# Turning the exponentials of attention tiles 6 to 11 by VectorE blocks and copies in a buffer of their own instead of by TensorE

## The chip, the cores and the metric

The kernel runs on one core of one Trainium2 chip. The metric is device time in microseconds, the median of repeated executions. Beside it there is one profiled execution, from which all rows below come. PE is TensorE, PEld its weight loads, DVE is VectorE, ACT is ScalarE, POOL is GpSimd, SP is SyncE, which starts the DMA transfers.

## What is computed

Three layers follow one another over 4608 tokens (8 batches of 576). All inputs are float32. Cut to what matters:

```python
k_p = k.reshape(B, H, Sp, 8, D).mean(axis=3)          # 72 pooled keys of 64 per head, 8 heads
v_p = v.reshape(B, H, Sp, 8, D).mean(axis=3)
scores = scale * (q @ k_p.T);  scores -= scores.max(-1)
attn = exp(scores);  attn /= attn.sum(-1) + 1e-09
x = (attn @ v_p)                                       # 4608 x 512

g = relu(x @ w_in) ** 2                                # 512 -> 2048
y = g @ w_out                                          # 2048 -> 512

logits = y @ phi                                       # 32 slots = 8 experts x 4
d = softmax(logits, over tokens);  slot_in = d.T @ y
slot_out[e] = relu(slot_in[e] @ w1[e]) @ w2[e]
out = softmax(logits, over slots) @ slot_out
```

## The kernel before

The tokens are cut into 36 tiles of 128. Work is written out in slots. A slot holds half a unit of the first product (`x @ w_in`): a unit is one tile and one quarter of the 2048 columns, twelve matmuls of line 492 in sequence, the high part of x, `xh`, times both parts of the weights and the low part, `xl`, times the high one. The function that emits a unit is `l1_steps`: twelve matmuls into a PSUM buffer of tag `l1` (two buffers), a relu on ScalarE out of PSUM into `r` (line 520), and a square, by VectorE from the PSUM buffer and `r` (line 528) or by ScalarE (line 530). The squared result `g` is stored to DRAM (line 532) and later read back in a turned form (line 572) for the logits (line 616) and their softmax (lines 658 to 743).

Attention of a tile is placed at slots fixed in advance, `attention(t, a_at[t])`: scores (`sc_steps`, matmuls of line 245, a row maximum by VectorE at line 253, and for most tiles eight exponentials with their sums by ScalarE at line 258), normalisation by VectorE (lines 285 to 287), turning (`att_aT` and `att_shift`, four and five slots behind the first), and the weighted sum (`av_steps`, line 340, then line 349 and line 351, which split it into `xh` and `xl`). The weighted sum takes the exponentials with the 72 keys in the partitions, `aT`, so that the normalised 128x(8x72) block `es` has to be turned for each of the eight heads. The kernel has two ways for this, and the set `EX` says which tiles take the second:

- by TensorE (`aT_steps`): eight transposes into PSUM (line 314), four heads in tag `gT` or `att` at a time, and two copies of 72x512 by ScalarE into `aT` (line 318);
- by blocks: VectorE turns all 32x32 blocks at once (line 328), reading `es` in columns of 96 for each head, into a 128x768 block; then twelve copies move the blocks to their places in `aT` (`att_shift`), by the pattern "VAVAVAAAVAVA" five of 32x256 and two of 8x256 on ScalarE (line 306), three and two on VectorE (line 308).

Tile pools hand out buffers: `aT` has one buffer, the 128x768 block lies in the last quarter of a `st1` buffer (`turned()[0]`). The other parts of that buffer and of `tmp` are five buffers for reloads of `g`, numbers 1 to 5 of the list `xbuf`. At the same time VectorE and ScalarE split the weights of the second matrix and pool keys and values; GpSimd pools them, too.

The order on each engine is made by the tile framework's scheduler from the slots and priorities, so that a change in one place can shift instructions of others.

Of the kernel before, what the change touches and what calls it, by code (L numbers as in the profile page):

```python
# [8 lines left out]
F32 = mybir.dt.float32  # L9
# [8 lines left out]
def kernel(  # L18
# [12 lines left out]
    nc = tc.nc  # L31
    B, H, S, D = q.shape
# [7 lines left out]
    P = 128  # L40
    NT = NTOK // P
# [29 lines left out]
    a1 = att_pools.enter_context(tc.tile_pool(name="a1", bufs=1))  # L71
# [217 lines left out]

    att_norm = whole(norm_steps)  # L290

    EX = range(12, NT)

    def att_shift(t):
        if t not in EX:
            return
        aT = aT_t[t] = a3.tile([SP, H, P], F32, tag="aT", name="aT")
        blk = turned()[0]
        for n in range(12):
            e = "VAVAVAAAVAVA"[n]  # L300
            r, m = n % 4, n // 4
            w = min(32, SP - 32 * m)
            dst = aT[32 * m:32 * m + w, :, 32 * r:32 * r + 32]
            src = blk[32 * r:32 * r + w, :, m]
            if e == "A":
                nc.scalar.copy(out=dst, in_=src)  # L306
            else:
                eng[e].tensor_copy(dst, src)  # L308

    def aT_steps(t, half):  # L310
        es = es_t[t]
        pa = ps("gT" if t in (0, 2, 4, 6, 8, 10, 12, 14, 16, 18, 20, 22, 24, 26, 28, 29, 30, 31, 33) else "att")
        for i in range(HH):
            nc.tensor.transpose(pa[:SP, i * P:(i + 1) * P], es[:, half * HH + i], ident)
        yield
        if t not in aT_t:
            aT_t[t] = a3.tile([SP, H, P], F32, tag="aT", name="aT")
        mark["aT", t] = nc.scalar.copy(
            out=aT_t[t][:, half * HH:(half + 1) * HH].rearrange("p h t -> p (h t)"), in_=pa[:SP]
        )  # L320
        yield

    def att_aT(t):
        if t in EX:
            es_t.pop(t)
            x = es2[t % 2]
            wide = bass.AP(tensor=x.tensor, offset=x.offset, ap=[list(x.ap[0]), [SP, H], [32, 3], [1, 32]])
            nc.vector.transpose(out=turned()[0], in_=wide)  # L328
            return
        for half in range(2):  # L330
            for _ in aT_steps(t, half):
                pass
# [212 lines left out]
            next(l1_t[t, j])  # L545

    xbuf, gT_at, g_back = [], {}, {}
    gT_free = [1, 2, 3, 4, 5]

    def turned():  # L550
        if not xbuf:
            x = stp.tile([P, 8, 512], F32, tag="st1", name="turned")
            xbuf.append(x[:, 6:8].rearrange("p a b -> p (a b)")[:, :H * 96].rearrange("p (h m i) -> p h m i", m=3, i=32))
            xbuf.extend(y[:, i:i + 2].rearrange("p a b -> p (a b)") for y, i in ((x, 0), (x, 2), (x, 4), (tmp, 0), (tmp, 2)))
        return xbuf

# [12 lines left out]
    def reload_turned(t, j):  # L569
        i = gT_at[t, j] = gT_free.pop(0)  # L570
        gc = gT_t[t, j] = turned()[i]
        nc.sync.dma_start(
            out=gc.rearrange("p (u f) -> p u f", u=2),
            in_=g_dram[t // 2][:, j].rearrange("u c (i s) f -> (c i) u (s f)", s=4),
        )
# [362 lines left out]
    def attention(t, a0):  # L938
        if t >= NT - 4:
            if t % 2 == 0:  # L940
                at(a0 - 2, pinned, "sq", turn_q, t)
            for n, fn in ((1, att_sc), (2, att_exp), (2, att_norm)):
                at(a0 + n, early, fn, t)
            n = (240, 242, 254, 259)[t - NT + 4]
            at(n - 2, early, att_aT, t)
            at(n - 1, early, att_shift, t)
            at(n, early, att_av, t)
            return
        if t < ND:
            at(a0, att_qT, t)  # L950
        elif t % 2 == 0:
            at(a0 - 2, pinned, "sq", turn_q, t)
        at(a0 + 1, att_sc, t)
        at(a0 + 2, att_exp, t)
        at(a0 + 2, att_norm, t)
        at(a0 + 4, att_aT, t)
        at(a0 + 5, att_shift, t)
        if a0 + 6 + t % 2 < 8 * ND + 14:
            at(a0 + 7, att_av, t)
        else:  # L960
            at(a0 + 6 + t % 2, pinned, "logits", att_av, t)
# [205 lines left out]
    for h in range(2):  # L1167
        cols = slice(h * QF // 2, (h + 1) * QF // 2)
        part = p2.tile([P, QF // 2], F32, tag="r", name="part")
        with tc.issue_after(mark["acc"].ins):  # L1170
            mark["acc"] = nc.vector.scalar_tensor_tensor(
                out=part, in0=acc[:, cols], scalar=scl, in1=dp[:, cols], op0=ALU.mult, op1=ALU.add
# [222 lines left out]
```

## Time and profile before

| | |
|---|---|
| median of 3 runs | 750.98 us (749.83 to 752.17) |
| the profiled execution | 751.86 us |
| its span, from first to last instruction | 750.1 us |
| mean granted clock of TensorE | 0.984 |
| TensorE busy | 715.6 us, 95% |
| VectorE busy | 524.3 us, 70% |
| ScalarE busy | 387.8 us, 52% |
| GpSimd busy | 136.5 us, 18% |

The busy times are those of the whole span. A busy share near 1 says that an engine has little room left, not that it is always the one waited for. A window cuts the span into stretches. In the chain of waits each piece was released by the one ahead of it, so that it shows who was waited for in each stretch. The granted clock is 1.00 at 2.4 GHz and 0.50 at 1.2 GHz.

### The profile page before, as it was taken

Reading aid. Unit: us, or ns where it says so; the run is one execution under the profiler, and the core shown is the slowest. Engines: PE = TensorE matmul, PEld = TensorE weight load, DVE = VectorE, ACT = ScalarE, POOL = GpSimd, SP = SyncE. Lnnn points to the kernel's source line nnn. Section 1 sums busy time; section 2 is a strip of 40 time slices with the busy share of each in tenths; the row PEclk is TensorE's granted clock in tenths of the full one; section 3 lists DMA queues with packets and bytes.
Section 4 is the critical chain, followed back from the end, with each engine's and each line's share of the span. In section 5 each row is a group of like instructions: output and inputs, shape, how many; then the busy total and the mean of one; then the engine's idle time right before and its main releaser. Section 6 shows DMA issues by size and latency. Waiting matters only on the chain.

```text
span 750.1 us, 13911 instructions
## 1 busy us (share of the span) xinstructions
PE 715.6 (95%) x4969; PEld 497.4 (66%) x4969; DVE 524.3 (70%) x1048; ACT 387.8 (52%) x1132; POOL 136.5 (18%) x151
## 2 busy tenths in 40 slices
PE   7799899999999999999999999999999999999985
PEld 7677678787776767666666656667666766764342
DVE  4998854497896788878979787778878574414132
ACT  3766767464656456346646462637466453333132
POOL 2234400004971400050342120320000000000000
PEclk9999999999999999999999999999999999999996
DMA  8967945658776996686998788879676434988998
GB/s 256 257 198 237 260 136 155 218 144 258 213 224 163 274 258 185 191 251 169 250 283 232 195 242 241 229 204 262 181 231 213 141 127 147 410 326 341 394 303 337
DMA packets 213012, 175.05 MB, mean 233 GB/s; under 512 B 75216, under 2 KB 169424, under 8 KB 212944
## 3 DMA queue, kind: packets, MB, share of 16 engines
q1 hardware_dynamic: 212944, 174.17, 75.7%
q8 instruction: 39, 0.64, 0.3%
q14 instruction: 29, 0.24, 0.1%
HBM read 126.94 MB, written 47.19 MB: 232 GB/s over the span
## 4 chain that ended last, share of the span: by engine, by line
PE 56%; DVE 19%; DMA 9%; ACT 6%; issue 5%; POOL 3%; SPq 1%; POOLq 0%; DVEq 0%; ACTq 0%
PE l L492 33%; PE misc L743 3%; ACT es L258 2%; DMA kv<-in_v_dram 2%; POOL w L429 2%; PE pl L616 2%; ACT aT L306 2%; DVE es L287 2%; DVE aT L308 2%; PE l L1228 2%; PE att L340 2%; DMA kv<-in_k_dram 2%; PE gT L340 2%; DMA tmp<-g_dram 1%; PE misc L1228 1%
## 5 line engine op out<-in xcount | busy, mean ns | idle before, releaser
L492 PE MATMUL l<-w,xh 128*128 128x512 f32 x1152 | 380.0, 409 | 4.4 <-DVE tmp L528 1.6
L492 PEld LDWEIGHTS l<-w,xh 128*128 128x128 f32 x1152 | 207.8, 189 | 70.3 <-issue 16.9
L492 PE MATMUL l<-w,xl 128*128 128x512 f32 x576 | 229.5, 400 | 0.3 <-DVE xl L351 0.3
L520 ACT ACTIVATE r<-l 128x512 f32<-128x512 f32 x142 | 85.6, 604 | 153.4 <-PE l L492 145.4
L492 PEld LDWEIGHTS l<-w,xl 128*128 128x128 f32 x576 | 108.4, 188 | 29.5 <-issue 4.2
L154 POOL TENSOR_TENSOR kv<-kv 72x512 f32<-72x512 f32 x40 | 53.9, 1350 | 221.5 <-DMA kv<-in_v_dram 115.2
L306 ACT COPY aT<-turned 32x256 f32<-32x256 f32 (+1 forms) x168 | 67.8, 404 | 25.5 <-DVE turned L328 22.7
L258 ACT ACTIVATE es<-att,mx 128x72 f32<-128x72 f32 x120 | 37.1, 336 | 24.1 <-DVE mx L253 23.7
L528 DVE TENSOR_TENSOR g<-l,r 128x512 f32<-128x512 f32 x55 | 37.5, 682 | 17.0 <-ACT r L520 10.8
L580 DVE STREAM_TRANSPOSE turned<-turned 128x1024 f32<-128x1024 f32 x39 | 47.5, 1229 | 1.9 <-DMA turned<-g_dram 1.8
L258 ACT ACTIVATE es<-gT,mx 128x72 f32<-128x72 f32 x120 | 36.7, 330 | 9.8 <-DVE mx L253 9.8
L308 DVE COPY aT<-turned 32x256 f32<-32x256 f32 (+1 forms) x120 | 40.5, 337 | 1.7
L429 POOL TENSOR_TENSOR w<-tmp,w 128x512 fp32r<-128x512 f32 x16 | 28.4, 1780 | 61.9 <-ACT w L427 53.2
L530 ACT ACTIVATE g<-r 128x512 f32<-128x512 f32 x54 | 34.4, 639 | 0.7
L528 DVE TENSOR_TENSOR tmp<-l,r 128x512 f32<-128x512 f32 x33 | 22.6, 684 | 17.1 <-ACT r L520 14.4
L287 DVE TENSOR_TENSOR es<-es,rs 128x576 f32<-128x576 f32 x36 | 33.3, 927 | 0.9
L580 DVE STREAM_TRANSPOSE tmp<-tmp 128x1024 f32<-128x1024 f32 x25 | 30.3, 1224 | 5.2 <-DMA tmp<-g_dram 5.2
L155 POOL TENSOR_TENSOR kv<-kv 72x256 f32<-72x256 f32 x40 | 33.6, 848 | 0.9
L374 ACT ACTIVATE tmp<-st 128x512 f32<-128x512 f32 x32 | 21.5, 676 | 14.9 <-DMA st<-in_moe_w_in_dram 10.0
L376 DVE TENSOR_SCALAR tmp<-tmp 128x512 uint32<-128x512 uint32 x32 | 15.5, 485 | 16.3 <-ACT tmp L374 16.3
L743 PE MATMUL misc<-g,d 128*32 128x512 f32 x134 | 25.7, 629 | 1.2 <-DVE d L730 0.7
L385 DVE SCALAR_TENSOR_TENSOR tmp<-st,tmp 128x512 f32<-128x512 uint32 x32 | 26.3, 824 | 0.6
(232 smaller groups left out, 1060.2 us busy)
## 6 DMA issues: line engine op xcount, KB each, us to landing
g_dram<-g SPq DMA_DIRECT2D x95, 256.0 KB
w<-in_moe_w_dram SPq DMA_DIRECT2D x44, 512.0 KB
turned<-g_dram SPq DMA_DIRECT2D x39, 512.0 KB
tmp<-g_dram SPq DMA_DIRECT2D x25, 512.0 KB
g_back<-g_dram SPq DMA_DIRECT2D x40, 256.0 KB
kv<-in_k_dram SPq DMA_DIRECT2D x32, 288.0 KB
kv<-in_v_dram SPq DMA_DIRECT2D x32, 288.0 KB
out_dram<-o SPq DMA_DIRECT2D x36, 256.0 KB
```

Source lines behind the costliest of these rows:

```text
L154: eng.tensor_tensor(out=x[:, :, 0:4], in0=x[:, :, 0:4], in1=x[:, :, 4:8], op=ALU.add)
L258: mark["es", t] = nc.scalar.activation(out=es[:, e], in_=sv[:, h], func=AF.Exp, bias=mx[:, e:e + 1], accum_out=rsum[:, t % 8, e, 0:1],)
L287: mark["norm", t] = nc.vector.tensor_tensor(out=es, in0=es, in1=rs.unsqueeze(2).to_broadcast([P, H, SP]), op=ALU.mult)
L306: nc.scalar.copy(out=dst, in_=src)
L308: eng[e].tensor_copy(dst, src)
L429: nc.gpsimd.tensor_tensor(out=w[kk][:, 1], in0=c, in1=w[kk][:, 0].bitcast(F32), op=ALU.subtract)
L492: mm = mark["l1", t, j] = nc.tensor.matmul(hp, steps[i][0], steps[i][1], start=(i == 0), stop=(i == n - 1))
L520: nc.scalar.activation(out=r, in_=hp, func=AF.Relu, scale=1.0 / (R * R if sq == "V" else R))
L528: mark["sq"] = nc.vector.tensor_tensor(out=dst, in0=pre, in1=src, op=ALU.mult)
L530: nc.scalar.activation(out=dst, in_=src, func=AF.Square)
L580: nc.vector.transpose(out=gc.rearrange("p (n i) -> p n i", i=32), in_=gc.rearrange("p (n f) -> p n f", f=32))
L743: mark["dg"] = nc.tensor.matmul(dp[32 * j:32 * j + 32], d[:, u], g if t < NT - 4 else natural(g), start=(u == 0), stop=(u == width(t) - 1),)
```

## The change

`EX` begins with tile 6 instead of tile 12, so that six more tiles take the second way. The 128x768 block gets a buffer of its own, `es_T`, 3 KB in each partition, out of the pool `a1`. The list `xbuf` loses its first entry, which the block was; the five buffers for reloads stay the same, under numbers 0 to 4. Line numbers from 293 to 552 are one higher in the changed kernel.

```diff
--- before.py
+++ after.py
@@ -289,13 +289,14 @@
 
     att_norm = whole(norm_steps)
 
-    EX = range(12, NT)
+    EX = range(6, NT)
+    es_T = a1.tile([P, H * 96], F32, tag="esT", name="esT").rearrange("p (h m i) -> p h m i", m=3, i=32)
 
     def att_shift(t):
         if t not in EX:
             return
         aT = aT_t[t] = a3.tile([SP, H, P], F32, tag="aT", name="aT")
-        blk = turned()[0]
+        blk = es_T
         for n in range(12):
             e = "VAVAVAAAVAVA"[n]
             r, m = n % 4, n // 4
@@ -325,7 +326,7 @@
             es_t.pop(t)
             x = es2[t % 2]
             wide = bass.AP(tensor=x.tensor, offset=x.offset, ap=[list(x.ap[0]), [SP, H], [32, 3], [1, 32]])
-            nc.vector.transpose(out=turned()[0], in_=wide)
+            nc.vector.transpose(out=es_T, in_=wide)
             return
         for half in range(2):
             for _ in aT_steps(t, half):
@@ -545,12 +546,11 @@
             next(l1_t[t, j])
 
     xbuf, gT_at, g_back = [], {}, {}
-    gT_free = [1, 2, 3, 4, 5]
+    gT_free = [0, 1, 2, 3, 4]
 
     def turned():
         if not xbuf:
             x = stp.tile([P, 8, 512], F32, tag="st1", name="turned")
-            xbuf.append(x[:, 6:8].rearrange("p a b -> p (a b)")[:, :H * 96].rearrange("p (h m i) -> p h m i", m=3, i=32))
             xbuf.extend(y[:, i:i + 2].rearrange("p a b -> p (a b)") for y, i in ((x, 0), (x, 2), (x, 4), (tmp, 0), (tmp, 2)))
         return xbuf
```

The first place is TensorE at tile 6, behind the scores of tile 7 (line 245); `es_121` holds the exponentials of tile 6, line 314 is the transposes, line 340 (341 in the changed kernel) the weighted sum. Before:

```order
L492 MATMUL l_1247<-w_251,xl 128x512
L245 MATMUL att<-kb_120,acc 128x144 x4
L314 MATMUL gT<-ident,es_121 72x128 x8
L492 MATMUL l_1340<-w_428,xh 128x512 x2
L492 MATMUL l_1340<-w_428,xl 128x512
```

And in the changed kernel:

```order
L493 MATMUL l_1248<-w_252,xl 128x512
L245 MATMUL att<-kb_120,acc 128x144 x4
L341 MATMUL gT<-aT,vp 64x128 x8
L493 MATMUL l_1342<-w_429,xh 128x512 x2
L493 MATMUL l_1342<-w_429,xl 128x512
```

The weighted sum of tile 6, which stood two units of the first product further on, moved to where the transposes stood.

The second place is ScalarE at tiles 12 and 13, the first tiles that were turned by blocks before; `es_121` is tile 12 and `es_122` tile 13, lines 306 and 307 the copies, lines 520 and 521 the relu. Before:

```order
L258 ACTIVATE es_121,rsum<-gT,mx 128x72 x8
L520 ACTIVATE r<-l_2396 128x512
L258 ACTIVATE es_122,rsum<-att,mx 128x72 x8
L453 COPY wt<-gT 128x512
L306 COPY aT<-turned 32x8x32 x5
L306 COPY aT<-turned 8x8x32 x2
L520 ACTIVATE r<-l_2439 128x512
L453 COPY wt<-gT 128x512
```

And in the changed kernel:

```order
L258 ACTIVATE es_121,rsum<-gT,mx 128x72 x8
L521 ACTIVATE r<-l_2403 128x512
L258 ACTIVATE es_122,rsum<-att,mx 128x72 x4
L454 COPY wt<-gT 128x512
L307 COPY aT<-esT 32x8x32 x5
L307 COPY aT<-esT 8x8x32 x2
L258 ACTIVATE es_122,rsum<-att,mx 128x72 x4
L521 ACTIVATE r<-l_2446 128x512
L521 ACTIVATE r<-l_2522 128x512
```

The copies of tile 12 moved ahead of four of tile 13's eight exponentials, and the relu of the next unit stands behind both.

The third place is TensorE late in the program, at one of the last weighted sums (line 340 before, 341 after); line 743 is the second product of the slot softmax, line 616 the logits. Before:

```order
L492 MATMUL l_6459<-w_765,xl 128x512
L340 MATMUL att<-aT,vp 64x128
L245 MATMUL att<-kb_120,qt 128x144
L340 MATMUL att<-aT,vp 64x128
L245 MATMUL att<-kb_120,qt 128x144
L340 MATMUL att<-aT,vp 64x128 x6
L743 MATMUL misc<-g,d 32x512 x2
L743 MATMUL misc<-tmp,d 32x512 x2
L743 MATMUL misc<-g,d 32x512 x3
L743 MATMUL misc<-tmp,d 32x512
L616 MATMUL pl<-turned,a_sb 32x256 x4
```

And in the changed kernel:

```order
L493 MATMUL l_6466<-w_766,xl 128x512
L743 MATMUL misc<-g,d 32x512 x2
L743 MATMUL misc<-tmp,d 32x512 x2
L743 MATMUL misc<-g,d 32x512 x3
L743 MATMUL misc<-tmp,d 32x512
L616 MATMUL pl<-turned,a_sb 32x256 x4
L341 MATMUL att<-aT,vp 64x128
L245 MATMUL att<-kb_120,qt 128x144
L341 MATMUL att<-aT,vp 64x128
L245 MATMUL att<-kb_120,qt 128x144
L341 MATMUL att<-aT,vp 64x128 x6
```

The matmuls of lines 743 and 616 moved from behind the weighted sum to ahead of it.

## Rows read from the trace of the kernel before

**Rows 1.** The page, busy time and share of the span of each engine.
```profile
PE 715.6 (95%) x4969; PEld 497.4 (66%) x4969; DVE 524.3 (70%) x1048; ACT 387.8 (52%) x1132; POOL 136.5 (18%) x151
```

**Rows 2.** Windows: stretch, length, busy us (x instructions) per engine, clock, DMA, GB/s.
```profile
130.00:150.00 20.00, 19.91 (x216) 15.10 (x215) 9.09 (x20) 9.48 (x19) 0.00 (x0) 1.00 0.65 205
150.00:170.00 20.00, 20.00 (x126) 16.91 (x125) 18.42 (x43) 13.62 (x49) 0.00 (x0) 1.00 0.52 144
170.00:190.00 20.00, 20.00 (x112) 14.81 (x111) 14.17 (x24) 9.14 (x35) 10.56 (x11) 1.00 0.86 273
190.00:210.00 20.00, 20.00 (x128) 15.12 (x126) 16.75 (x22) 11.38 (x28) 18.98 (x18) 1.00 0.77 209
210.00:230.00 20.00, 19.14 (x110) 15.34 (x109) 16.95 (x32) 14.15 (x51) 10.31 (x13) 1.00 0.63 173
230.00:260.00 30.00, 30.00 (x198) 22.38 (x200) 19.87 (x32) 12.52 (x31) 10.40 (x13) 1.00 0.83 249
```

**Rows 3.** The chain of waits, 60 to 260 us: start, us, what.
```profile
118.29 0.87 PE gT L314 x8
...
198.31 0.60 ACT r L520
...
217.59 1.93 ACT es L258 x12
...
223.51 0.98 DVE turned L328
...
228.57 0.66 PE gT L451 x4
```

**Rows 4.** Lines by form: what, xcount | busy us, mean ns | idle before, releaser.
```profile
L306 ACT COPY aT<-turned 32x256 f32<-32x256 f32 x120 | 48.5, 404 | 24.9 <-DVE turned L328 22.7 <-DVE rs L285 0.8
...
L308 DVE COPY aT<-turned 32x256 f32<-32x256 f32 x72 | 23.7, 329 | 0.9
L328 DVE STREAM_TRANSPOSE turned<-es 128x768 f32<-128x768 f32 x24 | 23.1, 964 | 0.7 <-ACT aT L306 0.2
...
L306 ACT COPY aT<-turned 8x256 f32<-8x256 f32 x48 | 19.3, 402 | 0.6
...
L308 DVE COPY aT<-turned 8x256 f32<-8x256 f32 x48 | 16.8, 350 | 0.8
...
L314 PE MATMUL gT<-ident,es 128*72 128x128 f32 x48 | 7.0, 290 | 3.2 <-DVE es L287 3.2
L318 ACT COPY aT<-gT 72x512 f32<-72x512 f32 x12 | 7.0, 594 | 1.0 <-PE gT L314 1.0
```

**Rows 5.** The timeline around tile 6: start, us, engine, instruction [idle before].
```profile
114.32 0.76 DVE L287 TENSOR_TENSOR es<-es,rs 128x576 f32<-128x576 f32 x1
...
118.13 1.04 PE L314 MATMUL gT<-ident,es 128*72 128x128 f32 x8
...
124.70 1.09 PE L340 MATMUL gT<-aT,vp 72*64 72x128 f32 x16
```

**Rows 6.** The timeline at tile 12, first VectorE, then ScalarE.
```profile
221.64 1.83 DVE L287 TENSOR_TENSOR es<-es,rs 128x576 f32<-128x576 f32 x1
...
224.52 2.90 ACT L306 COPY aT<-turned 32x256 f32<-32x256 f32 x7 [0.78 <-DVE rs L285]
```

**Rows 7.** Lines by form, VectorE alone, 220 to 260 us.
```profile
L308 DVE COPY aT<-turned 8x256 f32<-8x256 f32 x4 | 2.1, 534 | 0.1
```

**Rows 8.** Windows, the stretch in which TensorE's clock fell late.
```profile
600.00:608.00 8.00, 7.86 (x52) 3.94 (x53) 5.73 (x15) 3.23 (x14) 0.00 (x0) 0.79 0.19 60
```

**Rows 9.** The chain of waits, from 596 us on.
```profile
602.63 3.48 PE misc L743 x16
...
634.07 1.92 PE misc L743 x16
```

**Rows 10.** TensorE's waits, 560 to 640 us: waited for, us in total, times, longest.
```profile
PE att L340 <- ACT aT L306: 0.8, 1, 0.8
...
PE misc L743 <- DVE d L730: 0.4, 1, 0.4
```


## The prediction

> **What bounds the kernel now.** I read the page first: TensorE is busy for 95% of the span, VectorE for 70%, ScalarE for 52% [rows 1]. That makes TensorE the bound on average, and eight transposes taken off it ought to pay in full. The average hides the stretch that matters, so I cut the span into windows second. From 150 to 230 us TensorE is full (its only gap, 0.86 us, lies in the last window), but VectorE is also busy for 18.42 + 14.17 + 16.75 + 16.95 = 66.29 of 80 us; only from 230 to 260 does it fall to two thirds [rows 2]. Third comes the chain of waits. Up to 198 us it runs through TensorE alone, and the transposes of tiles 6 to 11 are pieces of it: the one at 118.29 us stands for all, 0.87 us for a tile, six tiles. At 198.31 it leaves TensorE by a relu on ScalarE and goes on through VectorE and ScalarE (exponentials of tile 12 at 217.59, its block transpose at 223.51) until TensorE, which had waited, goes on at 228.57 [rows 3]. The reader is to see that around 228 us the three engines are due at nearly the same time: what comes before on TensorE is worth its time only if VectorE and ScalarE get there earlier as well.
>
> **What it removes, adds and moves.** Each of the six tiles loses eight transposes on TensorE, 0.87 us in the chain [rows 3], so 6 x 0.87 = 5.2 us, and two ScalarE copies of 594 ns, 1.19 us [rows 4]. Each gains one VectorE block transpose of 964 ns, three VectorE copies of 329 ns and two of 350 ns, in sum 0.96 + 0.99 + 0.70 = 2.65 us, and on ScalarE five copies of 404 ns and two of 402 ns, 2.82 us, net +1.64 us [rows 4]. For six tiles that is -5.2 us of TensorE, +15.9 of VectorE, +9.8 of ScalarE.
>
> Tile 6 shows what one tile brings. Its normalised exponentials are done at 114.32 + 0.76 = 115.08 us, while TensorE turns them only at 118.13, and uses the result at 124.70 [rows 5]. In the changed order the eight weighted sums stand where the transposes stood. By then: 115.08 + 0.96 for the block transpose, + 2.90 for seven copies in a row [rows 6], makes 118.9, against 118.13 when TensorE gets there. It waits 0.8 us and gives back what tile 6 saved. The weighted sum of tile 7 comes in its old place, with time to spare, so about 0.9 us is kept there. From tile 8 on the inserted instructions delay others: on ScalarE the relu that frees a product's PSUM buffer stands behind seven copies, on VectorE the squares and subtractions stand behind a block transpose and five copies, and TensorE, with two buffers for these products, waits for both. I don't sum these waits one by one, since the meeting at 228 us decides about what is left.
>
> For that meeting: the work for tiles 6 and 7 falls before 150 us, where VectorE is busy for 9.09 of 20 us [rows 2]; its idle time hides their 5.3 us, and without that cover they would come on top of the sum below. Tiles 8 to 11 put 4 x 2.65 = 10.6 us on VectorE between 150 and 210 us. It is busy there for 18.42 + 14.17 + 16.75 = 49.34 of 60 us [rows 2], so its idle time is 10.66 us, just what the new work needs. Working without a gap it comes to tile 12's block transpose about when it did before, 223.51 [rows 3]; over the whole 80 us 66.29 + 10.6 = 76.9 leaves it 3.1 us at most by which it can be earlier. I take 223, since TensorE hands over its products somewhat earlier. Behind this transpose ScalarE does seven copies (2.90 us, [rows 6]) and then, which is new in its order, four exponentials of tile 13's second half before the relu that TensorE needs: 12 entries took 1.93 us [rows 3], so eight take 1.29. 223 + 0.98 + 2.90 + 1.29 + 0.60 for the relu is 228.8 us, the time at which TensorE went on before (228.57). **The gain left at this place is taken as 0**; bounds: 3.1 us, if VectorE's idle time is all that is left to win, and -1.2 us, if the five copies of each of these four tiles run beside GpSimd as slowly as the short ones did at 220 to 260 us (534 ns in place of 350, [rows 7]): 4 x 2 x 0.18 = 1.5 us, of which 0.3 is saved again by idle time elsewhere.
>
> After that the order on TensorE is that of before up to about 590 us, and VectorE has a third of its time free [rows 2], so that nothing is won or lost. At about 600 us the order differs once more. Before, the weighted sum of the last block waited 0.83 us for copies of ScalarE (0.8, [rows 10]), and the clock fell to 1.2 GHz behind it: granted 0.79 over 600 to 608 us [rows 8], and sixteen matmuls of line 743 took 3.48 us against 1.92 at 634 [rows 9], 1.56 more. In the changed order these sixteen and the eight logits matmuls stand ahead of the weighted sum, whose copies are then done. That takes away 0.83 + 1.56 = 2.4 us. Against it stands a wait of line 743 for its own input, since it comes earlier; it has one such wait of 0.4 us elsewhere [rows 10]. So 2.0 us, with bounds 0 (the wait only changes its name, and the clock falls again) and 2.4. The buffer of its own frees the block that tiles 12 and later had shared with the reloads; the loads at the end are started by TensorE's progress, and I cost this at nothing. It would cost what the loads are late if TensorE reached them first.
>
> **The sum.** 0 at 228 us and -2.0 us at 600 us. The profiled execution took 751.86 us, 0.88 above the median of the runs (750.98); differences go over unchanged: 751.86 - 2.0 = 749.9 for an execution like the profiled one, 750.98 - 2.0 = **749.0** for the median. Of 5.2 us taken from TensorE none would arrive through the edit itself.
>
> Two rules speak against the edit. The Trainium skill, in VectorE: DVE Perf Modes, section Rules for kernel authors, gives a 128x128 transpose to TensorE if a PSUM destination will do, and the 32x32 ones to VectorE. The rows agree on the price (0.87 us of TensorE against 2.65 of VectorE and 1.64 of ScalarE); the sum by this rule is rival three. The Trainium skill, in GPSIMD Engine Reference, section Specifications, says that GpSimd shares its SBUF interfaces with VectorE and that instructions with two SBUF inputs, or in a two-port mode, contend. The trace agrees: the normalisation of tile 12 took 1.83 us beside GpSimd [rows 6], 0.76 alone [rows 5]. By this rule the sum would be that of rival two, by the rows where GpSimd rests the forecast's.
>
> **Rivals.** One: VectorE keeps up. If ScalarE's copies fall into its idle time and VectorE drops all of its own, the 3.1 us at 228 us arrive, and the 2.0 at 600 with them: 750.98 - 5.1 = 745.9. For it speaks that ScalarE is busy for only 9 to 14 of each 20 us [rows 2]; against it, that tile 12's block transpose, copies and exponentials pass from one engine to the other, and each idles while the other works. Two, the slower side: VectorE misses the meeting. GpSimd is busy for 18.98 us of 190 to 210 [rows 2], where tiles 10 and 11 get their new work; the copies slow down as worked out, 1.2 us, TensorE stands still for some 3 us in one piece before 229 us, and its clock falls as at 600 us, another 1.56. With the late gain gone (the same wait of 0.8 in a new place) that is +2.8 us, 753.8. It decides when VectorE is later than 224.5 at tile 12. Against it: TensorE waited 0.86 us there before with the clock at full speed [rows 2]. Three: the transposes are hidden anyway and the late order brings nothing: 750.98, say 751.0. That the change doesn't do what it says is no rival, the instructions of tiles 6 to 11 are replaced one for one.
>
> **How the numbers follow.** Chances: forecast (747.9 to 750.3) 0.42; rival one (744.5 to 747.9) 0.25; rival three (750.3 to 751.9) 0.18; rival two (751.9 to 754.5) 0.15. About 0.3%, 2.25 us, is what a measurement of this kernel can tell from no change: faster is below 748.7, slower above 753.2. Faster takes all of rival one and some four tenths of the forecast's case: 0.25 + 0.17 = 0.42. Slower takes six tenths of rival two, 0.09. The rest, 0.49, is no change. The range leaves out a fifth of rival one below and a third of rival two above: 745.5 to 753.0.
>
> **What would show it.** Right: six fewer groups of eight transposes on TensorE, and new idle time on TensorE before 229 us, 3 us or more in the windows of 150 to 230, with VectorE above 75 of 80 us; the chain of waits there through VectorE and ScalarE; in the late stretch no wait of the weighted sum and a granted clock of 1.00. Wrong on the first term: TensorE without new waits there, everything after 230 us some 3 us earlier. Wrong on the second: a granted clock below 0.9 somewhere after 590 us again. The reader can test each by where the first matmul behind tile 12's copies starts (228.57 before).

## The result

The changed kernel takes 760.15 us (median of 5 runs, 759.54 to 760.68), the kernel before 750.98 us (749.83 to 753.22, 5 runs): a ratio of 1.0113, 95% interval 1.0091 to 1.0136. It is slower by 9.2 us, where a gain of 2 us was forecast with a range of 745.5 to 753.0. Its profiled execution took 759.55 us with a span of 757.8 us.

First comes the page of the changed kernel (the row that answers to [rows 1]) and the windows that answer to [rows 2]; the columns are those of these groups.

```profile
PE 713.3 (94%) x4921; PEld 495.2 (65%) x4921; DVE 538.2 (71%) x1084; ACT 398.6 (53%) x1162; POOL 136.5 (18%) x151
```

```profile
150.00:170.00 20.00, 18.74 (x112) 15.52 (x111) 17.71 (x43) 15.31 (x53) 0.00 (x0) 1.00 0.50 139
170.00:190.00 20.00, 20.00 (x107) 14.26 (x106) 18.78 (x36) 12.65 (x47) 10.13 (x11) 1.00 0.91 281
190.00:210.00 20.00, 17.56 (x89) 12.82 (x89) 19.65 (x27) 13.20 (x29) 15.89 (x17) 0.91 0.75 199
210.00:230.00 20.00, 19.41 (x118) 15.39 (x117) 18.16 (x33) 10.04 (x37) 11.85 (x14) 1.00 0.48 152
230.00:260.00 30.00, 27.91 (x179) 20.75 (x178) 15.51 (x31) 13.94 (x34) 6.09 (x8) 0.94 0.76 200
```

On average almost nothing happened: TensorE is busy for 2.3 us less, VectorE for 13.9 us more, ScalarE for 10.8 us more. In the windows TensorE, which had one gap of 0.86 us between 150 and 230 us, now has gaps of 1.26, 2.44 and 0.59 us there and 2.09 us behind, and its granted clock falls to 0.91 in 190 to 210 and to 0.94 in 230 to 260. VectorE is busy for 17.71 + 18.78 + 19.65 + 18.16 = 74.30 of 80 us in 150 to 230. What follows are TensorE's waits of the changed kernel in a timeline of TensorE alone: start, busy, instruction, and in brackets the idle time before it with what ended it.

```profile
119.36 1.09 PE L341 MATMUL gT<-aT,vp 72*64 72x128 f32 x16 [0.77 <-ACT aT L307]
...
168.26 0.73 PE L493 MATMUL l<-w,xh 128*128 128x512 f32 x2 [1.26 <-ACT r L521]
...
196.47 0.93 PE L493 MATMUL l<-w,xh 128*128 128x512 f32 x2 [2.44 <-DVE g L529]
...
214.36 1.08 PE L468 MATMUL misc<-s,at_sb 128*128 128x32 f32 x8 [0.59 <-DVE at_sb L462]
...
233.31 0.73 PE L493 MATMUL l<-w,xh 128*128 128x512 f32 x2 [2.09 <-ACT r L521]
```

The five waits add up to 7.15 us, against the one of 0.86 us before. Behind the waits of 2.44 and 2.09 us the granted clock falls: 0.91 over 20 us and 0.94 over 30 us are 1.8 us of full speed each. So 6.3 us of waits and 3.6 us of clock stand against what the missing transposes save.

To see where the 9 us come from, one can count: both kernels issue the same 1728 matmuls of the first product (line 492 before, 493 after). The table takes the start of the n-th of them (counted from 0) from the timelines and gives how much later (+) it comes than in the kernel before. All are set to 0 at the 216th, at 114 us, up to where TensorE's order is the same; the executions differ there by up to 4.4 us from their beginnings. The other columns belong to experiments below.

| matmul | us before | changed | t6_7 | t8_9 | t10_11 | less_pool | red10_11 | red_pin |
|---|---|---|---|---|---|---|---|---|
| 288 | 143.17 | -0.73 | -0.72 | -0.16 | -0.16 | -0.74 | -0.72 | -0.73 |
| 384 | 178.57 | -0.03 | -0.73 | +0.54 | -0.17 | -0.06 | -0.02 | -0.05 |
| 432 | 194.79 | +1.38 | -0.73 | +0.15 | +2.03 | -1.25 | -0.89 | -0.80 |
| 480 | 212.06 | +3.21 | -0.73 | +2.70 | +6.23 | -1.75 | -1.28 | -1.21 |
| 552 | 236.03 | +5.88 | -1.23 | +2.40 | +5.82 | -2.41 | +2.18 | -0.90 |
| 692 | 284.29 | +7.05 | -0.41 | +2.54 | +7.13 | -0.99 | +4.49 | +3.89 |
| 1016 | 405.92 | +6.48 | -0.96 | +1.65 | +4.99 | -2.07 | +4.58 | +3.44 |
| 1052 | 417.83 | +9.43 | -0.85 | +3.17 | +7.61 | -0.65 | +9.21 | +5.15 |
| 1520 | 594.99 | +9.47 | -0.65 | +2.56 | +7.85 | -0.87 | +8.71 | +5.57 |
| 1628 | 638.32 | +7.16 | -2.95 | +2.57 | +5.55 | -3.18 | +6.41 | +3.27 |
| 1700 | 665.86 | +7.11 | -2.99 | +2.57 | +5.51 | -3.22 | +6.36 | +3.23 |

The table follows one profiled execution of each kernel, which need not be near its median: red_pin's profiled execution took 756.38 us with a median of 759.22, red10_11's 763.34 with a median of 758.55.

The changed kernel gains 0.7 us with tiles 6 and 7, loses it again with tiles 8 and 9, and then loses 5.9 us from there to matmul 552, where tiles 10 to 13 are worked on. From 552 to 1052 some 3.6 us more go, in places that the edit doesn't touch, and about 2.3 come back late.

The cause of the largest piece is seen on VectorE and GpSimd. The timeline of VectorE at tiles 10 and 11 (x5 are a tile's five copies in a row), and of GpSimd at the same time:

```profile
189.23 0.97 DVE L329 STREAM_TRANSPOSE esT<-es 128x768 f32<-128x768 f32 x1
...
190.23 4.38 DVE L309 COPY aT<-esT 32x256 f32<-32x256 f32 x5
...
197.53 1.49 DVE L381 TENSOR_SCALAR tmp<-tmp 128x512 uint32<-128x512 uint32 x1
...
201.06 1.71 DVE L392 SCALAR_TENSOR_TENSOR st<-tmp 128x512 uint32<-128x512 uint32 x1
...
208.04 3.37 DVE L309 COPY aT<-esT 32x256 f32<-32x256 f32 x5
```

```profile
189.94 0.74 POOL L155 TENSOR_TENSOR kv<-kv 72x256 f32<-72x256 f32 x1
190.64 1.32 POOL L154 TENSOR_TENSOR kv<-kv 72x512 f32<-72x512 f32 x1
...
192.39 1.34 POOL L154 TENSOR_TENSOR kv<-kv 72x512 f32<-72x512 f32 x1
193.68 1.52 POOL L155 TENSOR_TENSOR kv<-kv 72x256 f32<-72x256 f32 x2
```

The five copies of tile 10 took 4.38 us and those of tile 11 3.37 us. By the rows on which the prediction rested ([rows 4]) they were to take 3 x 0.329 + 2 x 0.350 = 1.69 us. The pieces of the chain of waits show them one by one: start, duration, instruction.

```profile
190.25 0.57 DVE aT L309
190.84 1.28 DVE aT L309
192.12 0.46 DVE aT L309
192.59 1.28 DVE aT L309
193.89 0.74 DVE aT L309
...
208.33 1.28 DVE aT L309
```

Of tile 10's five, two took 1.28 us each, the time of one long GpSimd instruction (1.32 and 1.34 us in the rows above), in place of 0.28 to 0.35. The block transpose at 189.23, also beside GpSimd, took the 0.97 us that it takes elsewhere. Other instructions of VectorE are slow there, too: line 381 took 1.49 us at 197.53, line 392 1.71 at 201.06, against 0.41 and 0.68 in the quiet parts of the same timeline. That is so in the kernel before as well (its line 380 took 1.50 us at 204.78). What is new there is the copies.

### The profile page after: what moved, and what is told of

It is laid out like the page before. It is cut to its first block, busy times and chain, and to the rows that moved or that the text cites. A ratio compares the mean times of both kernels' runs of the same rounds, so it can differ in the third digit from the quotient of the medians.

```text
span 757.8 us, 13885 instructions
## 1 busy us (share of the span) xinstructions
PE 713.3 (94%) x4921; PEld 495.2 (65%) x4921; DVE 538.2 (71%) x1084; ACT 398.6 (53%) x1162; POOL 136.5 (18%) x151
## 4 chain that ended last, share of the span: by engine, by line
PE 55%; DVE 18%; ACT 8%; DMA 7%; issue 5%; POOL 4%; SPq 3%; POOLq 0%; DVEq 0%; ACTq 0%
PE l L493 33%; ACT es L258 3%; ACT aT L307 2%; PE misc L743 2%; PE pl L616 2%; POOL w L430 2%; DVE aT L309 2%; DMA kv<-in_k_dram 2%; PE l L1228 2%; DMA turned<-g_dram 2%; DVE es L287 2%; PE att L341 2%; DMA kv<-in_v_dram 2%; PE gT L341 1%; PE misc L1228 1%
## 5 line engine op out<-in xcount | busy, mean ns | idle before, releaser
L307 ACT COPY aT<-esT 32x256 f32<-32x256 f32 (+1 forms) x210 | 84.8, 404 | 25.9 <-DVE esT L329 23.3
L309 DVE COPY aT<-esT 32x256 f32<-32x256 f32 (+1 forms) x150 | 53.4, 356 | 2.4 <-PE gT L341 0.4
L529 DVE TENSOR_TENSOR tmp<-l,r 128x512 f32<-128x512 f32 x33 | 22.5, 683 | 16.6 <-ACT r L521 13.9
L155 POOL TENSOR_TENSOR kv<-kv 72x256 f32<-72x256 f32 x40 | 31.7, 800 | 0.9
L287 DVE TENSOR_TENSOR es<-es,rs 128x576 f32<-128x576 f32 x36 | 30.6, 852 | 0.9
L329 DVE STREAM_TRANSPOSE esT<-es 128x768 f32<-128x768 f32 x30 | 28.9, 963 | 0.4
L743 PE MATMUL misc<-g,d 128*32 128x512 f32 x134 | 24.1, 597 | 2.5 <-DVE d L730 2.0
```

The costliest lines, as they stand in the source:

```text
L287: mark["norm", t] = nc.vector.tensor_tensor(out=es, in0=es, in1=rs.unsqueeze(2).to_broadcast([P, H, SP]), op=ALU.mult)
L529: mark["sq"] = nc.vector.tensor_tensor(out=dst, in0=pre, in1=src, op=ALU.mult)
L743: mark["dg"] = nc.tensor.matmul(dp[32 * j:32 * j + 32], d[:, u], g if t < NT - 4 else natural(g), start=(u == 0), stop=(u == width(t) - 1),)
```

## Which tiles cost: the six taken apart

Theory one: VectorE's copies stand still beside GpSimd, and the loss comes from the tiles whose copies fall there (10 and 11; GpSimd is busy at 188 to 217 us). Theory two: the instructions are simply too many for VectorE and ScalarE, whichever tile they belong to. The edits differ in one line each:

```diff
-    EX = range(6, NT)
+    EX = [6, 7, *range(12, NT)]
```

and so with 8, 9 (t8_9), with 10, 11 (t10_11) and with 6 to 9 (t6to9).

Tiles 6 and 7 alone: 

> Only tiles 6 and 7 by blocks and copies of the six. GpSimd is idle at 110 to 150 us. Theory one (the loss comes from beside GpSimd): a gain of 0.7 us at 145 us as in the changed kernel, nothing lost at 160 to 235 us, 749.5 to 751.5 us. Theory two (number of instructions): two sixths of the loss, 753 to 755 us.

Measured: 749.70 us against 751.01 of the kernel before beside it, ratio 0.9991 (0.9964 to 1.0019).

Tiles 8 and 9 alone: 

> Only tiles 8 and 9 of the six. In the changed kernel TensorE came from 0.45 us ahead to 0.26 us behind over these tiles, behind a wait of 1.26 us for a relu. Theory one: 751 to 752.5 us. Theory two: 753 to 755 us.

Measured: 754.59 us against 751.01, ratio 1.0042 (1.0021 to 1.0063).

Tiles 10 and 11 alone: 

> Only tiles 10 and 11 by blocks and copies of the six. Theory one: most of the loss, 757 to 760 us, with a wait of TensorE of over 2 us behind tile 10's copies. Theory two: a third of it, 753 to 755 us.

Measured: 759.36 us against 751.58, ratio 1.0112 (1.0074 to 1.0149). The five copies took 3.60 and 4.88 us, and TensorE's waits are these (timeline of TensorE alone):

```profile
191.79 3.60 DVE L309 COPY aT<-esT 32x256 f32<-32x256 f32 x5
...
207.63 4.88 DVE L309 COPY aT<-esT 32x256 f32<-32x256 f32 x5
```

```profile
197.70 0.73 PE L493 MATMUL l<-w,xh 128*128 128x512 f32 x2 [2.81 <-ACT r L521]
...
206.47 0.73 PE L493 MATMUL l<-w,xh 128*128 128x512 f32 x2 [1.24 <-DVE g L529]
...
212.65 1.48 PE L341 MATMUL att<-aT,vp 72*64 72x128 f32 x16 [1.94 <-DVE aT L309]
```

Tiles 6 to 9: 

> Tiles 6 to 9 by blocks and copies, tiles 10 and 11 by TensorE again. Theory one (VectorE's copies stand still beside GpSimd, which works at 188 to 217 us, where tiles 10 and 11 get theirs): the loss comes from tiles 10 and 11, so 750 to 752 us here, and the five copies of every tile of the four take 1.5 to 1.8 us. Theory two (it is the plain number of instructions, 2.65 us on VectorE and 1.64 us on ScalarE for each tile): four sixths of the loss of 9.2 us, 756 to 758 us.

Measured: 754.84 us against 751.58, ratio 1.0059 (1.0034 to 1.0084).

Two tiles of six make most of the loss: tiles 10 and 11 alone cost 7.8 us where the whole change costs 9.2, and tiles 6 and 7, in a stretch in which GpSimd does nothing, cost nothing and may gain a little. That speaks for theory one. It doesn't hold fully: tiles 8 and 9 were to cost next to nothing by theory one and cost 3.6 us, the 753 to 755 us of theory two, although the five copies of each took the normal 1.46 us:

```profile
162.96 1.46 DVE L309 COPY aT<-esT 32x256 f32<-32x256 f32 x5
```

In the table this kernel is still 0.15 us late at matmul 432 and loses 2.5 us from there to 480, at 195 to 212 us, when its own copies are long done. TensorE waits for 0.24 and 0.57 us there. Another 1.0 us goes because the eight matmuls of line 460, which the kernel before does in one piece of 1.06 us, come in two pieces that take as long each (timeline of TensorE alone):

```profile
206.76 1.06 PE L460 MATMUL misc<-wt,phi_sb 128*32 128x512 f32 x6
...
209.34 1.05 PE L460 MATMUL misc<-wt,phi_sb 128*32 128x512 f32 x2
```

So a good part of the loss of tiles 8 and 9 lies in TensorE's own order. That tiles 8 and 9 leave VectorE work that is done later, beside GpSimd, where it is slower, may explain the waits; no run shows it. For t6to9 the middle of both forecasts came out (750 to 752 by one, 756 to 758 by the other), which agrees with t6_7 and t8_9 together.

## Less GpSimd

The direct test leaves VectorE as it is and takes GpSimd's long instructions away.

```diff
-        x = raw.pop((b, i))
+        x, c = raw.pop((b, i)), 8 if eng is nc.gpsimd and b in (3, 4) else D
...
-        eng.tensor_tensor(out=x[:, :, 0:4], in0=x[:, :, 0:4], in1=x[:, :, 4:8], op=ALU.add)
-        eng.tensor_tensor(out=x[:, :, 0:2], in0=x[:, :, 0:2], in1=x[:, :, 2:4], op=ALU.add)
+        eng.tensor_tensor(out=x[:, :, 0:4, :c], in0=x[:, :, 0:4, :c], in1=x[:, :, 4:8, :c], op=ALU.add)
+        eng.tensor_tensor(out=x[:, :, 0:2, :c], in0=x[:, :, 0:2, :c], in1=x[:, :, 2:4, :c], op=ALU.add)
```

In the changed kernel: 

> The changed kernel with GpSimd's two longer additions of batches 3 and 4 done on 8 of 64 columns: seven eighths of that pooling is left out, the order on VectorE is the same. Theory one: without the long GpSimd instructions the copies of tiles 10 and 11 take 1.5 us per five in place of 4.38 and 3.37, TensorE's wait of 2.44 us at 196 is gone, and the time is 750 to 753 us. Theory two: 757 to 760 us, as the changed kernel.

In the kernel before: 

> The kernel before with the same part of GpSimd's pooling left out, as what the run without long GpSimd instructions is to be held against. Both theories: 749 to 751 us; TensorE waits only 0.85 us at 228 because of VectorE, so not much more than that can be won.

Measured: 752.63 us for the changed kernel (ratio to the kernel before 1.0021, 1.0001 to 1.0040) and 751.54 us for the kernel before (0.9988, 0.9961 to 1.0015). VectorE's copies of tiles 10 and 11 and GpSimd's instructions at that time:

```profile
193.66 1.77 DVE L309 COPY aT<-esT 32x256 f32<-32x256 f32 x5
...
205.87 1.46 DVE L309 COPY aT<-esT 32x256 f32<-32x256 f32 x5
```

```profile
194.11 0.31 POOL L154 TENSOR_TENSOR kv<-kv 72x64 f32<-72x64 f32 x1 [9.01 <-DMA kv<-in_k_dram]
```

With the same instructions in the same order on VectorE the five copies take 1.77 and 1.46 us, the wait of 2.44 us at 196 us is gone, the clock stays at 1.00 from 110 to 240 us, and of the 9.2 us that the change costs 752.63 - 751.54 = 1.1 are left. So the loss comes from GpSimd's long instructions beside VectorE, not from the number of instructions alone. At matmul 552 this kernel is ahead by 2.4 us; the kernel before with the same work left out is ahead by 1.0 there. Even without GpSimd's long instructions the edit is worth 1.4 us by then, not 5.2 (TensorE still waits for 0.77, 1.23 and 0.31 us), and by the medians none of it is left at the end.

## Copies that don't stand still

GpSimd's work can't be left out, but the copies can be written so that they don't meet it. A maximum over one element moves the same data.

```diff
-                eng[e].tensor_copy(dst, src)
+                eng[e].reduce_max(out=dst, in_=src.unsqueeze(3), axis=AX.X) if t in (10, 11) else eng[e].tensor_copy(dst, src)
```

> The changed kernel, VectorE's five copies of tiles 10 and 11 written as maxima over one element, which move the same data. Theory one, in the form that a plain copy takes both of VectorE's ways into SBUF and stands still while GpSimd uses one: the five take 1.5 to 2 us in place of 4.38 and 3.37, TensorE's wait of 2.44 us at 196 is gone, 751 to 754 us. Rival (any VectorE instruction on these addresses is slow beside GpSimd): over 3 us for the five again, 758 to 760 us.

Measured: 758.55 us against 751.33, ratio 1.0093 (1.0061 to 1.0124), the time of the rival with the copies of theory one. The groups of line 309 by form: count, busy us and mean ns.

```profile
L309 DVE TENSOR_REDUCE aT<-esT 32x256 f32<-32x256 f32 x6 | 2.4, 406 | 0.1
...
L309 DVE TENSOR_REDUCE aT<-esT 8x256 f32<-8x256 f32 x4 | 1.6, 410 | 0.1
```

```profile
194.31 2.10 DVE L309 TENSOR_REDUCE aT<-esT 32x256 f32<-32x256 f32 x5
...
208.71 2.09 DVE L309 TENSOR_REDUCE aT<-esT 32x256 f32<-32x256 f32 x5
```

That the plain copy is what is slowed, and not any work on these addresses, is shown: beside GpSimd the maxima take 406 and 410 ns each, all alike, five in 2.10 us; copies by the same engine on the same addresses had taken up to 1.28 us. Alone, a copy of 32x256 takes 279 ns, so that beside GpSimd the order is turned round. The Trainium skill, in VectorE: DVE Perf Modes, section Mode 2×_2P — use both read ports for one tensor, has it that a copy of one source can read through both of VectorE's ports at once, and in the section Rules for kernel authors that `tensor_reduce` is to be expected at 1x, not in a faster mode; the Trainium skill, in GPSIMD Engine Reference, section Specifications, has it that GpSimd contends with the two-port modes. The rows agree with these pages. That the ports are the reason is not shown by a run here.

The time didn't follow. In the table the kernel recovers 4.5 us at matmul 480 (-1.28 against +3.21), then loses 3.5 us at tiles 12 and 13 and another 7 up to matmul 1052.

The other way round the same question is to give these copies to ScalarE:

```diff
-            e = "VAVAVAAAVAVA"[n]
+            e = "A" if t in (10, 11) else "VAVAVAAAVAVA"[n]
```

> The changed kernel with all twelve copies of tiles 10 and 11 on ScalarE. Theory one: ScalarE's copies keep 0.40 us beside GpSimd; VectorE loses 7.8 us of work, ScalarE gains 4; 752 to 755 us. Theory two (number of instructions): the work only changes its engine, 757 to 760 us.

Measured: 761.31 us against 751.33, ratio 1.0131 (1.0089 to 1.0173). The first part of it was right: twelve copies on ScalarE took 4.98 us, 0.42 each, beside GpSimd.

```profile
206.01 4.98 ACT L307 COPY aT<-esT 32x256 f32<-32x256 f32 x12
```

But the median is no better. At matmul 552 this kernel is 2.3 us late, where the changed kernel is 5.9; from there to 1052 it loses 7.3 us more. Up to 552 it loses in a new place: the block has one buffer, so that tile 11's transpose waits until ScalarE has moved all of tile 10; VectorE stands idle for 2.23 us there, and its later work still falls beside GpSimd. TensorE waits 2.06 us for it at another place (line 468, at 212.45), and the clock falls there (0.91 over 210 to 230). That the stalls of the copies are all of it, theory one in its plain form, falls with this run and the one before. Both recover some of the loss at tiles 10 to 13 and lose about 7 us behind 236 us.

Maxima for all tiles, in both kernels:

```diff
-                eng[e].tensor_copy(dst, src)
+                eng[e].reduce_max(out=dst, in_=src.unsqueeze(3), axis=AX.X)
```

In the changed kernel: 

> The changed kernel with VectorE's five copies of every tile from 6 on written as maxima over one element. Theory one: as with tiles 10 and 11 alone, and up to 2 us better where GpSimd works later on: 749 to 753 us. Rival: 758 to 760 us.

In the kernel before: 

> The kernel before with VectorE's copies of tiles 12 and later written as maxima over one element. Theory one: copies beside GpSimd drop from up to 1.3 us to 0.4, TensorE waits for few of them: 749 to 751 us. Rival: no change of the copies, 751 us.

Measured: 760.66 us (ratio 1.0101, 1.0047 to 1.0156) and 762.64 us (1.0149, 1.0103 to 1.0196), both misses of theory one. In the kernel before nothing differs up to 236 us (-0.9 us at matmul 552), and 11 us are lost behind it, with an order on the engines that the scheduler changed. Since the order changed as well, these two runs don't tell what the slower copy costs by itself.

## Tiles 12 and 13: the order on ScalarE

The 3.5 us that are left at matmuls 480 to 552 with fast copies stand where the prediction saw a long way: seven copies and four exponentials on ScalarE ahead of a relu. To tell whether this order makes them, tile 12's copies were held behind tile 13's last exponential, as in the kernel before.

```diff
-        at(a0 + 5, att_shift, t)
+        at(a0 + 5, pinned, ("es", 13), att_shift, t) if t == 12 else at(a0 + 5, att_shift, t)
```

With fast copies at tiles 10 and 11: 

> The same with VectorE's copies of tiles 10 and 11 as maxima over one element (2.1 us for five beside GpSimd). If ScalarE's order makes the 3.4 us that are left between 212 and 236 us: at most 1 us is left there, and the time is 754 to 756 us. If not: 758 us as without the hold.

Without: 

> The changed kernel with tile 12's copies held behind the last exponential of tile 13 on ScalarE, as in the kernel before. If the order on ScalarE makes the loss at tiles 12 and 13: TensorE's wait of 2.09 us at 233 falls below 1 us and the loss between 212 and 236 us from 2.7 to 1 us or less, time 757 to 758. If VectorE is simply late there: the wait stays at 2 us or moves to tile 12's weighted sum, 760 us.

And the changed kernel once more, for what belongs to the program and what to one execution: 

> The changed kernel once more. If the 3.0 us between 410 and 420 us and the 1.2 us between 270 and 284 us belong to the program, they are there again, and the time is 759 to 761 us. If they are chance of one execution, the profile shows other places.

Measured, against 752.92 of the kernel before beside them: red_pin 759.22 us (1.0078, 1.0043 to 1.0114; runs from 752.57 to 763.82), pin12 760.33 us (1.0107, 1.0065 to 1.0149), the repeat 760.97 us (1.0095, 1.0063 to 1.0127).

With both edits the loss at tiles 12 and 13 is gone: from matmul 480 to 552 red_pin goes from -1.21 to -0.90, red10_11 from -1.28 to +2.18. So this loss is made by ScalarE's order, as far as one execution of each tells. With slow copies it does the same there (0.9 us lost from 480 to 552 in place of 2.7), but pin12 came to matmul 480 later, 4.45 us against 3.21, and the median, 760.33, is not below that of the changed kernel: a miss of 2 to 3 us.

And again the time didn't follow: red_pin is 0.9 us ahead at 236 us and 3.9 us late at 284, with a granted clock of 0.88 over 270 to 284 us. TensorE's waits there, and VectorE's for transfers in the same stretch (timelines of one engine; 260.44 and the like are VectorE's turning of what was read back from DRAM):

```profile
276.00 1.09 PE L341 MATMUL att<-aT,vp 72*64 72x128 f32 x16 [1.89 <-DVE aT L309]
...
278.76 1.07 PE L743 MATMUL misc<-g,d 128*32 128x512 f32 x2 [1.10 <-DVE d L730]
```

```profile
260.44 1.25 DVE L580 STREAM_TRANSPOSE tmp<-tmp 128x1024 f32<-128x1024 f32 x1 [0.84 <-DMA tmp<-g_dram]
...
270.36 1.25 DVE L580 STREAM_TRANSPOSE turned<-turned 128x1024 f32<-128x1024 f32 x1 [2.84 <-DMA turned<-g_dram]
...
273.25 1.25 DVE L580 STREAM_TRANSPOSE turned<-turned 128x1024 f32<-128x1024 f32 x1 [0.79 <-DMA turned<-g_dram]
```

VectorE waits 0.84, 2.84 and 0.79 us for reloads of `g`; in the kernel before it waits once for one in this stretch, 0.55 us. In the chain of waits of this kernel the store ahead of them takes 9.32 us and a reload 5.82:

```profile
247.13 9.32 DMA g_dram<-tmp
...
267.34 5.82 DMA turned<-g_dram
```

## What is left behind 236 us

The changed kernel loses 1.2 us from matmul 552 to 692 (up to 284 us) and 3.0 us at 410 to 420 us; the repeat loses 1.7 and 3.6 us there, so these places belong to the program. VectorE waits for reloads of `g` (line 580): 9.4 us for those into `turned` and 2.6 us for those into `tmp`, before 1.8 and 5.2.

```profile
L580 DVE STREAM_TRANSPOSE turned<-turned 128x1024 f32<-128x1024 f32 x39 | 47.6, 1230 | 9.5 <-DMA turned<-g_dram 9.4
```

The sum of these waits, 12.0 us against 7.0, doesn't explain the time: in less_pool it is 12.3 us, and that kernel loses only 1.8 us from matmul 552 to 1052. Red10_11, act10_11 and red_pin lose 6 to 7 us there; why is open.

One candidate for the 3.0 us is GpSimd's pooling, behind which SyncE's queue stood before it issued a reload. It was taken for the pooling of batch 5, and that was shortened alone, with the edit of the section on less GpSimd and `b == 5`:

> The changed kernel with GpSimd's two longer additions of batch 5 alone on 8 of 64 columns (seven eighths of that pooling left out). It is for the 3.0 us that the changed kernel loses at 410 to 420 us: if GpSimd's pooling of this batch holds up SyncE's queue there, the reload of g behind it is issued earlier, the wait of 2.8 us at 420 goes and the time is 757 us; if the transfers themselves came late, the loss stays and it is 760 us.

Measured: 761.98 us against 751.01 (1.0137, 1.0084 to 1.0190). The loss at 410 to 420 us stayed, 4.3 us from matmul 1016 to 1052. But the run doesn't test the candidate. The additions that it shortened lie at 258 to 340 us; those ahead of this reload belong to the next batch and are as long as before, and SyncE waits 5.6 us for GpSimd there, where the changed kernel waits 5.7. One of them in less_pool5:

```profile
398.05 1.28 POOL L154 TENSOR_TENSOR kv<-kv 72x512 f32<-72x512 f32 x1 [0.27 <-DMA kv<-in_k_dram]
```

In the changed kernel the chain of waits runs from GpSimd's pooling through SyncE's queue and the reload to TensorE (start, us, what):

```profile
399.20 1.28 POOL kv L154
...
404.80 0.33 SPq L147
...
406.86 7.05 DMA turned<-g_dram
...
420.38 3.06 PE l L493 x12
```

The repeat has the same chain. In the kernel before SyncE waits for GpSimd, too (5.6 us), and issues its reloads 9.4 us earlier (at 396.76 us in place of 406.20), while TensorE comes to matmul 1016 only 6.8 us earlier. So the candidate is not ruled out, and which step makes the loss stays open.

The buffer alone was tried as well, with `EX = range(12, NT)`: 

> The block's buffer of its own alone, tiles 6 to 11 by TensorE as before. Both theories: no change, 750 to 752 us; if the late part of the program waits for less because of the buffer, TensorE does not wait 0.83 us at 600 us, and 748 to 750 us.

Measured: 751.63 us against 751.01, ratio 0.9995 (0.9966 to 1.0025), no difference. TensorE waits the same 0.8 us at 600 us, but the clock behind it stays at full speed:

```profile
PE att L341 <- ACT aT L307: 0.8, 1, 0.8
```

```profile
598.00:610.00 12.00, 11.16 (x74) 7.35 (x73) 9.15 (x24) 6.58 (x21) 0.00 (x0) 1.00 0.18 51
```

In before_less_pool, which has the order of the kernel before, the clock stays at 1.00 there as well; in t8_9, with the same wait, it falls (0.88 over 600 to 608 us). So the fall of the clock in [rows 8] belongs to single executions, and the order of instructions alone doesn't decide it.

## Why the prediction was wrong, step by step

- What bounds the kernel: right. TensorE, VectorE and ScalarE are due together at 228 us, and what TensorE saved before is worth nothing unless VectorE gets there earlier. VectorE was to be above 75 of 80 us busy in 150 to 230; it was 74.3, and the chain of waits from 188 to 233 us runs mostly through VectorE and ScalarE. New idle time of 3 us or more was to show on TensorE; it was 4.3 in these windows. These signs came nearly as named with a time 11 us off, since rival two would have shown them as well.
- Tiles 6 and 7: right. A wait of 0.8 us was worked out at tile 6, and 0.77 was measured; 0.9 us were to be kept, 0.7 were.
- **The term that failed is the gain left at 228 us.** It was taken as 0 with a lower end of -1.2 us, and it was -5.9 (at matmul 552). The step that failed is the cost of VectorE's copies beside GpSimd. The term charged 1.69 us for a tile's five copies, and its lower end 0.18 us more for each short one, 1.5 us in all. That came from a mean of 534 ns over four copies in [rows 7], of which three ran while GpSimd rested for all or nearly all of their time and took 0.28 us each, and one beside it took 1.28; single copies take 1.28 us beside a long GpSimd instruction, those of 32x256 too, and two tiles' copies cost (4.38 + 3.37) - 2 x 1.69 = 4.4 us, in the stretch where GpSimd rests least. VectorE reaches tile 12's block transpose at 226.8 us instead of 223 (0.3 of it since this execution began later). The chain of waits of the changed kernel there:

```profile
226.80 0.89 DVE esT L329
...
232.28 0.98 ACT r L521 x2
233.31 4.61 PE l L493 x12
```

- Behind this, ScalarE's order (seven copies, four exponentials, a relu) was seen and priced, 223 + 5.8 = 228.8. With 226.8 in its place the same sum gives 232.6, and the two relus ended at 233.26. The mechanism was right, its starting point was 3.8 us off. The first matmul behind tile 12's copies, which the prediction named as the test, starts at 233.31 us in place of 228.57.
- The clock was priced in rival two alone. It fell twice, behind the waits of 2.44 and 2.09 us, 1.8 us of full speed each. Rival two had the place, the cause and the clock, and its own condition came true (VectorE later than 224.5 at tile 12: 226.8); it was given 0.15 and 753.8 us because the slowdown was sized by the same mean.
- "Nothing is won or lost" behind 230 us: wrong. 3.6 us more were lost (from +5.88 at matmul 552 to +9.47 at 1520), all of it by 420 us, in front of reloads that come later. The prediction looked at engines there and not at transfers.
- The late term, -2.0 us: the size was met (from +9.47 to +7.16, 2.3 us), mostly by luck. 1.7 us of it came to own_buffer and before_less_pool too, which have the order of the kernel before: that part is a fall of the clock in the one execution that the rows were read from. What is left for the order is 0.6 us.
- The range: rival two is said to lie by six tenths above 753.2 us and by a third above 753.0, which can't both hold. The measured time lies far above either bound.

## What to carry to other kernels

Before work is moved to VectorE, look at what GpSimd does at that place in the program, instruction by instruction: a mean over a whole run, or over a window in which GpSimd rests part of the time, hides that a single copy can take as long as a whole GpSimd instruction. A saving on the engine that is busiest on average counts only where the next engine has room in the same stretch, and here the next two had too little. When one cause is taken away and the time stays, as with the maxima, look for the next place that is late before giving the theory up. And see in the trace whether an experiment changed the instructions that it was meant for: less_pool5 did not.

## What was not expected of the hardware

- Copies of 32x256 and 8x256 from SBUF to SBUF on VectorE take 0.28 us alone and, at tiles 10 and 11, up to 1.28 us beside GpSimd's additions of 1.28 to 1.34 us; block transposes (0.97 us) and maxima over one element (0.41 us) do not change.
- A wait of TensorE of 0.83 us at 600 us was followed by a fall of the clock in the profiled execution of the kernel before (granted 0.79 over 8 us) and in that of t8_9 (0.88), and by none in two others with the same wait (own_buffer, before_less_pool).
- The kernel before with maxima in place of VectorE's copies (0.40 and 0.41 us each in the mean, against 0.33 and 0.35) is 11.3 us slower as a whole (762.64 against 751.33), all of it behind 236 us. The order on the engines changed with them, so how much of this the slower instruction makes isn't shown.
